# Loading chunks and weight tiles as two transfers, of partitions 0 to 119 and of 120 to 127

## The chip, the cores and the metric

The kernel runs on one core of one Trainium2 chip. The metric is the device time of one execution in microseconds (us), lower being better. Engine names are those of the profile: PE is TensorE (PEld its weight loads), DVE VectorE, ACT ScalarE, POOL GpSimd, SP SyncE, whose queue (SPq) issues every transfer of this kernel.

## What is computed

A retention layer (linear attention with a decay per head) over 4 sequences of 768 tokens with 8 heads of 64 feeds a gated feed-forward layer with a convolution of width 3:

```python
for t in range(S):                       # 768 steps, per batch and head
    state = gamma * state + outer(k[t], v[t])
    y[t] = q[t] @ state / sqrt(D)
x = y, heads side by side                # 4 x 768 x 512
h = maximum(x @ w_in, 0)                 # 512 -> 1024
conv_out[s] = sum over k of conv_w[k] * h[s + k - 1]
out = (h * sigmoid(conv_out)) @ w_out    # 1024 -> 512
```

All inputs are float32, and the two weight matrices and conv_w are float64, which the host passes as pairs of 32-bit words.

## The kernel before, in words

**Retention in chunks.** The 768 steps are cut into 12 chunks of 64 tokens; two sequences are done at a time, so there are 24 chunks in all (`n`, 0 to 23). One chunk's q, k (in two layouts) and v for two sequences and eight heads lie in a tile `rw` of 128 partitions, of which there are three. Chunks 0 to 4 are loaded in two transfers of 512 KB (`load`, L493, for q and k; `load_kv`, L497, for k and v), the later ones in one of 1 MB (L493). For a chunk, PE makes the scores (`scores`), DVE masks them (`masked`, L571), v is scaled by powers of the decay (`scale_v`: DVE at L521 or, for most chunks, ACT at L518), PE makes output and state (`mix`, all PE work of this part is at L551), ACT copies the state back (`carry`, L578), and DVE and ACT make the two halves of x, a rounded part and a rest (`decay` L585, `x_head` L595, `x_rest` L601).

**Weights.** The 16 tiles of w_in and w_out (512 KB each) and conv_w come as float64 words (`load_w`, L611) into one of four `g` tiles. ACT and DVE turn the words into two float32 parts by integer operations (`w_abs` L629 to `w_add` L710).

**Feed-forward.** For each of 12 units of 128 tokens (two sequences), `mm1` (L724) makes h from x and w_in in three products, `relu` (ACT, L733) moves it out of PSUM, DVE and ACT do the convolution and the gate (L749 to L775), and `mm2` (L789) multiplies by w_out. The result goes out by L802, 256 KB at a time.

**What sets the order.** `plan` walks through a list of tasks with estimated durations before anything is emitted and fixes the order of all instructions on each engine. It holds some transfers back so that not too many bytes queue at once (`QUEUE`, `HOLD`): such a load gets a dependency on a finished instruction of another engine (`held`, `add_manual_dep`). SP issues its transfers strictly in that order; one that waits keeps all behind it waiting. Between the tasks PE runs small filler products (`keep_warm`, L470) where the plan expects a gap. PE's own program is 37 pages of 256 instructions, which the chip fetches while the kernel runs; `Tensor.fetch` in the plan is a model of that.

**Completion counters.** Each transfer reports its landing on one of eight counters, taken in turn (DMAHW0 to DMAHW7 in the rows below). An instruction that reads the data waits for that counter, and a transfer that takes a counter again waits until the transfer that had it before has landed.

Of the kernel before, what the change touches and what calls it, by code (L numbers as in the profile page):

```python
# [11 lines left out]
I32 = mybir.dt.int32  # L12
# [32 lines left out]


PE, DVE, ACT, POOL, DMA = "PE", "DVE", "ACT", "Pool", "DMA"
ISSUE, FIRST_BYTE, SLOW_UNTIL, SLOW_BYTE, BYTE = 430, 1350, 5300, 1 / 250, 1 / 360

LANDING = {DMA: 1550, PE: 190, DVE: 130, ACT: 150, POOL: 150}  # L50
# [374 lines left out]
def retention_then_gated_ffn(  # L425
# [10 lines left out]
    nc = tc.nc  # L436
# [19 lines left out]
    def buf(name, shape, dtype=F32):  # L456
        return pool.tile(shape, dtype, name=name, bufs=BUFS[name])

    def ps_buf(name, shape=(P, 512)):
        return psum.tile(list(shape), F32, name=name, bufs=BUFS[name])  # L460
# [5 lines left out]
    def keep_warm(k):  # L466

        ps = ps_buf("ps_o")
        for i in range(k):
            nc.tensor.matmul(ps[:, : 2 * P], warm, warm.unsqueeze(1).broadcast_to([P, 2, P]), start=True, stop=True)  # L470
# [9 lines left out]
    rw, s_ps, st_ps, y_ps, xt, xs = {}, {}, {}, {}, {}, {}  # L480

    flat = lambda a: a.rearrange("p a b g c -> p a (b g c)")
    gy_0, gf, gv, mask_sb = (
        consts_sb[:, i:j].rearrange("p (a c) -> p a c", a=a) for (i, j), a in zip(CONSTS, (NPAIR, NC, NC, 1))
    )

    @emits
    def load(n):


        rw[n] = buf("rw", [P, 5, 2, NPAIR, C])
        slots = slice(0, 2 if n < ALONE else 4)
        nc.sync.dma_start(flat(rw[n][:, slots]), qkv[n][:, slots])  # L493

    @emits
    def load_kv(n):
        nc.sync.dma_start(flat(rw[n][:, 2:4]), qkv[n][:, 2:4])  # L497

    @emits
    def load_consts():  # L500
# [106 lines left out]
    @emits  # L607
    def load_w(i):
        n, src = (NF * 3, conv_w) if i == CONV else (512, w_in[i] if i < NF else w_out[i - NF])
        t = const.tile([P, 2 * n], F32, name="cw_t") if i == CONV else buf("g", [P, 2 * n])  # L610
        nc.sync.dma_start(t.bitcast(I32), src.bitcast(I32))  # L611
        t = t.rearrange("p (n w) -> p n w", w=2)
        pieces[i] = [t[:, :, 0].bitcast(I32), t[:, :, 1].bitcast(I32)]

# [189 lines left out]
    start, more, behind = plan(list_tasks())  # L804
    run_empty(WARM_UP)
    made = {}
    for k in sorted(start, key=start.get):
        if k in more:
            keep_warm(more[k])
        emit[k[0]](*k[1:])  # L810
        made[k] = nc.cur_bb.bb.instructions[-1]
        if k in behind:
            tc.add_manual_dep(
                made[k], made[behind[k]].name,
                mybir.DependencyInfo(mybir.DependencyClass.Sync, mybir.DependencyReason.DATA), reason="held back",
            )

# [50 lines left out]
```

## Time and profile before

| what | value |
|---|---|
| median of 3 runs | 351.71 us (351.38 to 360.04) |
| profiled execution | 356.1 us, its span 354.4 us |
| mean granted clock | 0.995 |
| busy: PE, PEld, DVE, ACT, POOL | 339.3, 304.9, 250.0, 207.8, 44.8 us |
| transfers | 10368 packets, 40.09 MB, 32.1% of the 16 engines' span |
| HBM read, written | 33.79 MB, 6.29 MB |

A span is the time from the first to the last instruction. Busy time is the sum of an engine's instructions; what an engine waited for is listed by line, total, number of times and longest. Transfers are listed by queue: q1 carries the kernel's data, q8 and q14 carry instructions. The median time from issue to landing stands at the end of each row of transfers. A window view gives, for each stretch, its length and then for each engine the busy time and the number of instructions, and after these the granted clock, the share of the DMA engines and GB/s.

### The profile page before, as it was taken

What the parts mean: (1) busy time and instruction counts of PE and PEld (TensorE: products, weight loads), DVE (VectorE), ACT (ScalarE), POOL (GpSimd) and SP (SyncE); (2) the same over time, 40 slices, a digit from 0 to 9 for tenths busy, and PEclk for the clock granted to TensorE, in tenths of its full rate; (3) what the DMA queues carried; (4) which work ended last, traced back from release to release, by engine and by line L of the source; (5) the groups of instructions that cost most, each with busy time, mean ns of one, the idle gap of its engine ahead of it and who ended that gap; (6) DMA issues with size and microseconds to landing.
All of it is one profiled execution on the core that took longest, in us unless ns stands there. A gap on an engine that the chain in (4) does not pass through costs nothing.

```text
span 354.4 us, 10912 instructions
## 1 busy us (share of the span) xinstructions
PE 339.3 (96%) x4763; PEld 304.9 (86%) x4763; DVE 250.0 (71%) x488; ACT 207.8 (59%) x418; POOL 44.8 (13%) x100
## 2 busy tenths in 40 slices
PE   6968999799999999999999999999999999999996
PEld 4857988799998899889888898999898888888886
DVE  3677999659999997566565675665656465999930
ACT  1255675596565887577466446446455555887831
POOL 0000000003999411000000000000000000000000
PEclk9999999899999999999999999999999999999999
DMA  7878898633020263305314334001001000100111
GB/s 249 329 254 277 283 350 308 249 120 117 18 106 0 75 227 111 100 33 179 99 42 164 120 120 148 34 2 59 4 0 62 0 31 30 61 30 31 61 59 59
DMA packets 10415, 40.78 MB, mean 115 GB/s; under 512 B 1280, under 2 KB 1664, under 8 KB 7936
## 3 DMA queue, kind: packets, MB, share of 16 engines
q1 hardware_dynamic: 10368, 40.09, 32.1%
q8 instruction: 37, 0.61, 0.7%
q14 instruction: 10, 0.08, 0.1%
HBM read 33.79 MB, written 6.29 MB: 113 GB/s over the span
## 4 chain that ended last, share of the span: by engine, by line
PE 79%; DVE 12%; issue 4%; ACT 2%; DMA 2%; SPq 0%; ACTq 0%; DVEq 0%
PE ps_o L789 35%; PE ps_m L724 30%; PE ps_y L551 5%; PE ps_st L551 4%; PE ps_s L551 4%; DVE cv L754 3%; DMA rw<-in_qkv 2%; DVE m L695 1%; DVE m L647 1%; DVE g L663 1%; DVE h L710 1%; DVE g L775 1%; DVE cv L765 1%; DVE g L655 1%; PE ps_o L470 1%
## 5 line engine op out<-in xcount | busy, mean ns | idle before, releaser
L724 PE MATMUL ps_m<-xu,wi_hi 128*128 128x256 f32 x768 | 141.6, 284 | 2.4 <-issue 2.0
L789 PE MATMUL ps_o<-h,g 128*128 128x512 f32 (+1 forms) x600 | 142.7, 386 | 0.0
L724 PEld LDWEIGHTS ps_m<-xu,wi_hi 128*128 128x128 f32 x768 | 121.4, 190 | 6.7 <-issue 0.8
L789 PEld LDWEIGHTS ps_o<-h,g 128*128 128x128 f32 x600 | 105.6, 188 | 20.0
L724 PE MATMUL ps_m<-xu,wi_lo 128*128 128x256 f32 x384 | 107.9, 281 | 0.7 <-issue 0.7
L754 DVE SCALAR_TENSOR_TENSOR cv<-h,cw_sb,cv 128x256 f32<-128x256 f32 x192 | 81.5, 480 | 16.2 <-ACT cv L749 16.2
L724 PEld LDWEIGHTS ps_m<-xu,wi_lo 128*128 128x128 f32 x384 | 72.9, 190 | 2.1 <-issue 2.1
L740 POOL COPY h<-h 128x4 f32<-128x4 f32 x80 | 43.8, 586 | 239.0 <-ACT h L733 239.0
L749 ACT ACTIVATE cv<-h,cw_sb 128x256 f32<-128x256 f32 x96 | 44.2, 503 | 18.0 <-DVE g L775 17.5
L775 DVE TENSOR_TENSOR g<-cv,g 128x512 fp32r<-128x512 f32 x48 | 33.2, 691 | 28.6 <-ACT g L770 28.3
L551 PE MATMUL ps_y<-rw 64*64 64x64 f32 x1472 | 50.2, 222 | 2.8 <-issue 2.8
L551 PEld LDWEIGHTS ps_y<-rw 64*64 64x64 f32 x1472 | 46.4, 136 | 3.9 <-issue 3.9
L760 ACT ACTIVATE cv<-cv 128x512 f32<-128x512 f32 x48 | 30.3, 632 | 24.6 <-DVE cv L754 24.5
L770 ACT CAST g<-cv 128x512 fp32r<-128x512 f32 x48 | 29.8, 621 | 24.8 <-PE ps_o L789 20.8
L765 DVE TENSOR_TENSOR cv<-h,cv 128x512 f32<-128x512 f32 x48 | 33.1, 689 | 14.4 <-ACT cv L760 13.9
L733 ACT ACTIVATE h<-ps_m 128x512 f32<-128x512 f32 x48 | 28.5, 594 | 14.6 <-PE ps_m L724 14.6
L551 PE MATMUL ps_s<-rw 64*64 64x64 f32 x768 | 29.4, 230 | 4.2 <-DMA rw<-in_qkv 2.3
L551 PEld LDWEIGHTS ps_s<-rw 64*64 64x64 f32 x768 | 26.9, 146 | 6.5 <-issue 2.4
L551 PEld LDWEIGHTS ps_st<-rw 64*64 64x64 f32 x704 | 23.8, 139 | 5.5 <-issue 3.8
L551 PE MATMUL ps_st<-rw 64*64 64x64 f32 x704 | 27.5, 226 | 0.8 <-issue 0.8
L571 DVE TENSOR_TENSOR rw<-ps_s,consts_sb 128x512 f32<-128x512 f32 x24 | 16.5, 689 | 13.4 <-PE ps_y L551 7.4
L518 ACT ACTIVATE rw<-rw,consts_sb 128x128 f32<-128x128 f32 x72 | 23.0, 392 | 4.0 <-DMA rw<-in_qkv 4.0
(39 smaller groups left out, 182.1 us busy)
## 6 DMA issues: line engine op xcount, KB each, us to landing
rw<-in_qkv SPq DMA_DIRECT2D x19, 1024.0 KB, 5.4
out_y<-o_sb SPq DMA_DIRECT2D x23, 256.0 KB, 2.0
rw<-in_qkv SPq DMA_DIRECT2D x10, 512.0 KB, 5.6
g<-in_w_in SPq DMA_DIRECT2D x8, 512.0 KB, 5.8
g<-in_w_out SPq DMA_DIRECT2D x8, 512.0 KB, 4.6
out_y<-o_sb SPq DMA_DIRECT2D x2, 128.0 KB, 1.7
consts_sb<-in_consts SPq DMA_DIRECT2D x1, 208.0 KB, 4.7
cw_t<-in_conv_w SPq DMA_DIRECT2D x1, 24.0 KB, 4.8
```

The source lines that it names most:

```text
L518: nc.scalar.activation(v[:, :, g], v[:, :, g], AF.Copy, scale=by[:, g : g + 1])
L551: nc.tensor.matmul(out, lhsT, rhs, start=start, stop=stop, skip_group_check=True)
L724: nc.tensor.matmul(h_ps[u, p][:, odd], w[:, k, fs], x[:, k].rearrange("p b t -> p (b t)"), start=(i == 0), stop=(i == len(products) - 1),)
L733: nc.scalar.activation(hs[u, p][:, :, :, 1 : P + 1], ps, AF.Relu)
L740: nc.gpsimd.tensor_copy(column(u, to), column(u + du, frm))
L749: nc.scalar.activation(cvs[u, p][:, i], hs[u, p][:, i, :, 1 : P + 1], AF.Copy, scale=cw_sb[:, f, 1:2])
L754: nc.vector.scalar_tensor_tensor(out=cv, in0=h[:, :, k : k + P], scalar=cw_sb[:, f, k : k + 1], in1=cv, op0=ALU.mult, op1=ALU.add)
L760: nc.scalar.activation(cvs[u, p], cvs[u, p], AF.Sigmoid)
L765: nc.vector.tensor_tensor(out=cv, in0=hs.pop((u, p))[:, :, :, 1 : P + 1], in1=cv, op=ALU.mult)
L770: nc.scalar.copy(gs[u, p][:, 0], cvs[u, p])
L775: nc.vector.tensor_tensor(out=lo, in0=cvs.pop((u, p)), in1=hi.bitcast(F32), op=ALU.subtract)
L789: nc.tensor.matmul(ps, g, w[f][:, cs], start=(f == 0 and i == 0), stop=(f == NF - 1 and i == 2))
```

## The change

Each load of a chunk (`load`, `load_kv`) and each load of a weight tile or of conv_w (`load_w`) becomes two transfers: one of partitions 0 to 119 and, right behind it on SP, one of partitions 120 to 127. The constants' load and the stores stay whole. The dependency of a load that is held back goes to the first of the two. The plan isn't told: its durations, and so the order of the tasks, stay.

```diff
+MOST = 120
...
+    def bring(to, src):
+
+        nc.sync.dma_start(to[:MOST], src[:MOST])
+        nc.sync.dma_start(to[MOST:], src[MOST:])
+
...
-        nc.sync.dma_start(flat(rw[n][:, slots]), qkv[n][:, slots])
+        bring(flat(rw[n][:, slots]), qkv[n][:, slots])
...
-        nc.sync.dma_start(flat(rw[n][:, 2:4]), qkv[n][:, 2:4])
+        bring(flat(rw[n][:, 2:4]), qkv[n][:, 2:4])
...
-        nc.sync.dma_start(t.bitcast(I32), src.bitcast(I32))
+        bring(t.bitcast(I32), src.bitcast(I32))
...
+        before = len(nc.cur_bb.bb.instructions)
         emit[k[0]](*k[1:])
         made[k] = nc.cur_bb.bb.instructions[-1]
         if k in behind:
             tc.add_manual_dep(
-                made[k], made[behind[k]].name,
+                nc.cur_bb.bb.instructions[before], made[behind[k]].name,
```

On SP, the start of the program before (a row is a line, the operation, the tiles and the shape; behind it the counters or engines that it waits for; the suffix _49 is part of a counter's name):

```order
1 L493 DMA rw<-in_qkv 128x1024
2 L501 DMA consts_sb<-in_consts 128x416
3 L497 DMA rw<-in_qkv 128x1024
4 L493 DMA rw<-in_qkv 128x1024
5 L497 DMA rw<-in_qkv 128x1024
6 L493 DMA rw<-in_qkv 128x1024
7 L497 DMA rw<-in_qkv 128x1024 [waits DVE_49]
```

The same place with the change, up to chunk 2's second load:

```order
1 L490 DMA rw<-in_qkv 120x1024
2 L491 DMA rw<-in_qkv 8x1024
3 L507 DMA consts_sb<-in_consts 128x416
4 L490 DMA rw<-in_qkv 120x1024
5 L491 DMA rw<-in_qkv 8x1024
6 L490 DMA rw<-in_qkv 120x1024
7 L491 DMA rw<-in_qkv 8x1024
8 L490 DMA rw<-in_qkv 120x1024
9 L491 DMA rw<-in_qkv 8x1024 [waits DMAHW0_49]
10 L490 DMA rw<-in_qkv 120x1024 [waits DMAHW1_49]
11 L491 DMA rw<-in_qkv 8x1024 [waits DMAHW2_49]
12 L490 DMA rw<-in_qkv 120x1024 [waits DMAHW3_49,DVE_49]
```

The order of the loads is the same, but the eight counters are used up with the first piece of chunk 1's second load, before with the first weight tile: row 9 waits for the first piece of chunk 0, row 11 for the constants.

On PE, the first scores before:

```order
107 L470 MATMUL ps_o<-o_sb 128x256
108 L551 MATMUL ps_s<-rw 64x64 [waits DMAHW0_49]
109 L551 MATMUL ps_s<-rw 64x64 x15
110 L470 MATMUL ps_o<-o_sb 128x256 [waits PE_49]
111 L551 MATMUL ps_s<-rw 64x64 [waits DMAHW3_49,DVE_49]
```

and with the change:

```order
107 L471 MATMUL ps_o<-o_sb 128x256
108 L557 MATMUL ps_s<-rw 64x64 [waits DMAHW0_49]
109 L557 MATMUL ps_s<-rw 64x64 [waits DMAHW1_49]
110 L557 MATMUL ps_s<-rw 64x64 x14
111 L471 MATMUL ps_o<-o_sb 128x256 [waits PE_49]
112 L557 MATMUL ps_s<-rw 64x64 [waits DMAHW5_49,DVE_49]
113 L557 MATMUL ps_s<-rw 64x64 [waits DMAHW6_49]
```

No instruction of PE, DVE, ACT or POOL changes its place; the readers of a loaded tile wait for two counters instead of one.

## The prediction

> **What bounds the kernel now.** The page comes first, for the engine that is full.
>
> ```profile
> span 354.4 us, 10912 instructions
> PE 339.3 (96%) x4763; PEld 304.9 (86%) x4763; DVE 250.0 (71%) x488; ACT 207.8 (59%) x418; POOL 44.8 (13%) x100
> PE 79%; DVE 12%; issue 4%; ACT 2%; DMA 2%; SPq 0%; ACTq 0%; DVEq 0%
> ```
>
> TensorE is busy for 339.3 of 354.4 us, and the third line, the chain that ended last, lies on it for 79%. So a change in transfers can only act where PE is idle or slow. Busy time by stage shows where that is (columns: PE, PEld, DVE, ACT, POOL, the granted clock, DMA share, GB/s).
>
> ```profile
> 0.00:66.00 66.00, 54.58 (x1495) 49.59 (x1496) 50.37 (x96) 34.64 (x76) 2.06 (x14) 1.00 0.84 289
> 66.00:70.00 4.00, 3.85 (x20) 3.85 (x20) 2.26 (x6) 1.15 (x3) 0.00 (x0) 0.57 0.80 324
> 70.00:125.00 55.00, 54.82 (x683) 51.45 (x681) 50.29 (x103) 37.37 (x75) 33.36 (x26) 1.00 0.23 77
> 125.00:355.00 230.00, 226.07 (x2572) 200.06 (x2568) 147.06 (x286) 134.59 (x266) 9.39 (x60) 1.00 0.20 70
> ```
>
> In the first 66 us PE lacks 11.4 us and the DMA share is 0.84; from 70 us on PE lacks about 0.2 us in 55 and the transfers take a fifth of the engines. The case is decided before 70 us. What PE waited for there (total, times, longest):
>
> ```profile
> PE ps_y L551 <- issue: 2.8, 5, 1.0
> PE ps_m L724 <- issue: 2.7, 2, 2.0
> PE ps_s L551 <- DMA rw<-in_qkv: 2.3, 2, 1.6
> PE ps_s L551 <- issue: 1.9, 1, 1.9
> PE ps_st L551 <- issue: 0.8, 1, 0.8
> ```
>
> Only 2.3 us are waits for a load. "issue" is time in which PE waited for nothing that the profile shows: 2.8 + 2.7 + 1.9 + 0.8 = 8.2 us in nine waits, all before 66.2 us. The longest has a sequel (a row of the chain, then the mm1 line in two windows):
>
> ```profile
> 64.18 1.97 issue
> 66.14:69.70 3.56, 3.56 (x18) 3.55 (x18) 0.52 0.85 343
> 69.70:71.70 2.00, 2.00 (x19) 2.00 (x19) 1.00 0.01 4
> ```
>
> After 1.97 us of nothing the granted clock is 0.52 for 3.56 us: 18 matmuls in 3.56 us, then 19 in 2.00 us. At full clock the 18 would have taken 18 x 2.00 / 19 = 1.90, so the sequel costs 1.7 us.
>
> The "issue" waits look like code arriving late. The DMA view of the first 66 us:
>
> ```profile
> GB/s 0 231 200 379 372 422 360 338 233 320 325 211 243 214 179 392 397 286 206 397 204 258 362 211 241 267 269 281 370 335 390 382 271 320 241 330 348 350 248 181
> DMA packets 4369, 19.08 MB, mean 289 GB/s; under 512 B 608, under 2 KB 736, under 8 KB 3424
> q1 hardware_dynamic: 4356, 18.88, 82.5%
> q8 instruction: 11, 0.18, 1.0%
> rw<-in_qkv SPq DMA_DIRECT2D x8, 1024.0 KB, 7.0
> g<-in_w_in SPq DMA_DIRECT2D x8, 512.0 KB, 5.8
> consts_sb<-in_consts SPq DMA_DIRECT2D x1, 208.0 KB, 4.7
> ```
>
> The last three rows give the loads' sizes and the us from issue to landing. Queue q8 carried 11 instruction packets of 0.18 MB / 11, about 16 KB each, while the loads kept the engines 82.5% busy. That both share engines is seen late in the run, where stores are alone but for such a packet: three windows, of 288 to 296, 268 to 273 and 304 to 308 us.
>
> ```profile
> out_y<-o_sb SPq DMA_DIRECT2D x2, 256.0 KB, 2.0
> ...
> q8 instruction: 1, 0.02, 1.5%
> out_y<-o_sb SPq DMA_DIRECT2D x1, 256.0 KB, 3.0
> ...
> q8 instruction: 1, 0.02, 2.1%
> out_y<-o_sb SPq DMA_DIRECT2D x1, 256.0 KB, 4.0
> ```
>
> A store lands in 2.0 us; with one code packet beside it, in 3.0 and 4.0. So a code packet and the rows of a data transfer queue for the same engine, and behind loads the packet is the late one. The rows do not say which engine that is.
>
> **The change part by part.** First, **the issues**. 46 loads become 92 issues.
>
> ```profile
> 0.73 0.38 SPq L493 DMA_DIRECT2D rw<-in_qkv  x1
> 1.17 0.42 SPq L501 DMA_DIRECT2D consts_sb<-in_consts  x1
> 2.11 0.43 SPq L493 DMA_DIRECT2D rw<-in_qkv  x1
> 3.08 0.71 SPq L493 DMA_DIRECT2D rw<-in_qkv  x1
> 2.11 6.97 DMA rw<-in_qkv
> 37.43 1.63 SPq L611 DMA_DIRECT2D g<-in_w_in  x2
> 42.19 2.88 SPq L611 DMA_DIRECT2D g<-in_w_in  x2
> 50.55 0.68 ACT L629 ACTIVATE m<-g 128x512 f32<-128x512 f32 x1 [1.03 <-DVE g L655]
> ```
>
> Back-to-back issues stand (2.11 - 1.17) / 2 = 0.47 us apart, with chunk 0's second load between these two. Later, SP's idle time hides the extra 46. At the start nothing does: the second piece of the first load goes out at 1.17 instead of 0.73, so the first scores are 0 to 0.47 us later; I take 0.3, since the first piece is still moving then. Chunk 1's load, the chain's 6.97 us, has three more issues up to its end, 1.4 us; the 1.2 MB queued ahead of it (at 231 GB/s some 5 us) hide those, and without that cover they cost 1.4.
>
> **The counters.** Each transfer takes the next of eight completion counters and waits for the one eight back, now four loads back instead of eight. Chunk 2's second piece waits for the constants, which landed at 1.17 + 4.7 = 5.9, so it leaves about 3 us later than chunk 2's load did at 3.08; the 2.3 MB ahead of it are still moving then and hide that. The load of weight tile 6 at 42.19 now waits for that of 37.43 to land, 5.8 us at the median: 43.2, 1 us late, with SP's next loads queued behind it. ACT first reads tile 6 at 50.55, which hides it. I take 0 for both, and 1.0 as the upper bound.
>
> **The rows per engine.** A load of 128 rows gives 16 engines 8 rows each. A 120-row piece gives its busiest engine at least 8 (over 16 or 15 engines), 15 if it gets only 8 engines; the 8-row piece adds one row to some of them. So a load's busiest engine carries 9 rows at best, 16 at worst: 9/8 to 2 times the wire time. By how the bytes are cut I take 9/8. 512 KB at the best slice, 422 GB/s, are 1.24 us, so the ninth row is 0.16 us, and 0.31 us for 1 MB. The first 66 us' share becomes 82.5 x 9/8 = 93%, still under full. Who waits for a load, beside PE's two waits above:
>
> ```profile
> ACT rw L518 <- DMA rw<-in_qkv: 4.0, 2, 2.3
> ACT m L629 <- DMA g<-in_w_in: 1.7, 1, 1.7
> ```
>
> Five waits at 0.16 to 0.31 each are 0.8 to 1.6 us, up to 2.8 if the queue at 93% adds almost as much again; some lie beside PE work. I take 1.4, bounds 0 and 2.8.
>
> The Trainium skill ("DMA: Bandwidth & Descriptors", on why a DMA increments its semaphore by 16) says that the engines used are the largest number up to 16 that divides the rows, the lowest-numbered ones: 15 for 120 rows, 8 for 8 rows. By that rule the factor is 9/8 and one engine gets no load at all; no run here shows it yet, since every transfer in this trace has 128 rows.
>
> **The code.** If code's engine still carries loads, its packets stand behind 8 or 9 rows per load. With 9, and one or two loads ahead, each of the nine waits grows by 0.16 to 0.62 us, 1.4 to 5.6 in all; with 8, by 0. I take 1.0, nearer to the lower end, as no more than about half of the loaded engines have a ninth row.
>
> The sum: 0.3 + 0 + 1.4 + 1.0 = 2.7 us. The profiled execution took 356.1 us for its span of 354.4, and becomes 358.8; it stands 4.4 us above the median of the runs, 351.7, which becomes **354.4 us**. With all lower ends it is 351.7, with all upper ones 351.7 + 0.47 + 1.0 + 2.8 + 5.6 = 361.6.
>
> **The rivals.** *Faster: the engine left without loads is the one code comes through.* Then the nine waits and the half clock go: 8.2 + 1.7 = 9.9 us. Against it: the loads still land later (+1.7 us), and DVE has little room to follow:
>
> ```profile
> 40.00:50.00 10.00, 9.85 (x288) 9.31 (x278) 9.20 (x21) 7.09 (x17) 0.68 (x5) 1.00 0.89 290
> ```
>
> With 9.20 of 10 us busy on DVE, that stretch can shrink by under 1 us. I take 2.5 us given back in all: 351.7 - 9.9 + 1.7 + 2.5 = 346.0, between 341.8 and 350. Its chance: the split may leave 0 to 8 engines of 16 without loads, 4 on average, so one in four holds the code's.
>
> *Slower: the pieces move at a worse rate than whole loads.* 19.08 MB at 422 GB/s need 45 us of the first 66, so there is room for a factor of 66 / 45 = 1.46. Above it the loads set the pace of the first stage, and the code waits vanish inside it. At 1.75 it takes 79 us, +13: 365; at 2, the end of the bound, 90 us, +24: 376. For it: 16 rows on the busiest engine, or two engines that write to the same part of SBUF and halve each other, whatever the count. Against it: in this trace 16 engines reach 422 GB/s together, but on whole loads alone.
>
> The Trainium skill ("SBUF — State Buffer", on the DMA port swizzle) says that DMA bandwidth depends on how many of 16 SBUF ports the partitions reach, four neighbouring partitions sharing one. By that rule the 8 last rows reach two ports, four engines to each, and the 120 rows may pair up too, which is a factor around or over 1.5 and so this rival's 360 to 376. The trace can't say: with 128 rows all its loads move alike.
>
> *The split changes nothing that matters*: if both pieces spread as the whole did, only the issue cost stays: 352.
>
> **How the numbers follow.** Forecast 0.40, faster rival 0.27, slower rival 0.28, no effect 0.05. Runs of this kernel differ by about 2%, so within 2% is 344.7 to 358.7. Faster: rather more than half of the faster rival, 0.15, and 0.03 for what I have not seen: 0.18. Slower: nearly all of the slower rival, 0.27, and a fifth of the forecast, 0.08: 0.35. The rest, 0.47, is within. Alone, the forecast has 351.7 to 361.6. Cases of both signs hold most of the chance, so the range reaches from 344 (about 0.1 below) to 375 (about 0.1 above).
>
> **What would show it.** Right: about nine "issue" waits of PE before 66 us summing to 8 to 13 us, a half clock near 66 us, loads landing 0.2 to 0.8 us later than 5.8 to 7.0, GB/s slices still near 400. The faster rival: "issue" waits under 2 us and a clock of 1.00 throughout. The slower one: GB/s in the first 66 us that never pass some 280, a DMA share over 0.95, and PE, ACT and DVE waiting for loads by over 10 us. The forecast is wrong if the q8 packets come on time though loads land late, or if SP's counter waits show up as PE waits for loads.

## The result, and the profile after

| | before | after |
|---|---|---|
| median of 4 runs | 352.73 us (351.38 to 360.04) | 377.24 us (373.54 to 382.74) |
| profiled span | 354.4 us | 375.2 us |
| mean granted clock | 0.995 | 0.977 |

The ratio is 1.067, with a 95% interval of 1.056 to 1.079. The kernel is slower by some 24 us. Each time given here and below is the median of all runs, slow ones among them, while a ratio and its interval compare the fast runs alone. The forecast was 354.4 us with a range of 344 to 375, so it was wrong; the time is that of the slower rival at its upper end, 376.

The page comes first again. Its transfer rows are shown too, with the number of packets by size.

```profile
span 375.2 us, 10990 instructions
PE 347.1 (92%) x4763; PEld 311.6 (83%) x4763; DVE 249.8 (67%) x488; ACT 204.8 (55%) x418; POOL 45.6 (12%) x100
DMA packets 10738, 40.79 MB, mean 109 GB/s; under 512 B 1602, under 2 KB 1986, under 8 KB 8258
q1 hardware_dynamic: 10690, 40.09, 43.0%
PE 70%; DMA 16%; DVE 5%; issue 4%; ACT 3%; SPq 1%; ACTq 0%; DVEq 0%
```

The bytes are the same, 40.09 MB, but they keep the DMA engines busy for 43.0% of a longer span, before for 32.1%. On the chain that ended last, transfers went from 2% to 16%, PE from 79% to 70% and DVE from 12% to 5%. Busy time by stage shows where (columns: stretch, length, PE, PEld, DVE, ACT, POOL, granted clock, DMA share, GB/s).

```profile
0.00:66.00 66.00, 48.08 (x1061) 43.22 (x1061) 36.19 (x65) 22.74 (x49) 0.66 (x8) 0.90 0.92 211
66.00:70.00 4.00, 2.96 (x134) 2.75 (x134) 2.57 (x6) 3.13 (x8) 0.40 (x3) 1.00 0.95 220
70.00:90.00 20.00, 14.15 (x323) 13.11 (x323) 14.34 (x31) 9.55 (x22) 0.43 (x3) 0.95 0.95 235
90.00:125.00 35.00, 35.00 (x401) 34.64 (x401) 29.42 (x60) 21.61 (x43) 18.39 (x13) 0.98 0.45 118
145.00:375.00 230.00, 227.03 (x2608) 200.99 (x2600) 147.27 (x288) 132.91 (x267) 9.54 (x60) 1.00 0.28 72
```

The last 230 us hold 227.03 us of PE work, before 226.07: nothing was lost there. The first stage, the one full of loads, ended near 66 us and now lasts to about 90. In its first 66 us the transfers move 211 GB/s instead of 289, with a DMA share of 0.92 instead of 0.84. More time on the DMA engines and fewer bytes: each transfer takes longer, and the DMA engines do not stand idle for want of transfers. The DMA view of the same 66 us (the first row is GB/s in 40 slices; the loads' rows end in KB and median us to landing):

```profile
GB/s 0 206 211 244 238 221 228 223 228 221 221 226 233 226 228 231 223 228 223 233 209 221 149 246 228 243 209 213 194 134 218 199 190 229 227 181 211 171 233 226
DMA packets 3565, 13.90 MB, mean 211 GB/s; under 512 B 653, under 2 KB 781, under 8 KB 3029
q1 hardware_dynamic: 3556, 13.76, 90.6%
q8 instruction: 8, 0.13, 1.0%
rw<-in_qkv SPq DMA_DIRECT2D x10, 480.0 KB, 9.6
rw<-in_qkv SPq DMA_DIRECT2D x5, 960.0 KB, 12.3
g<-in_w_in SPq DMA_DIRECT2D x8, 480.0 KB, 9.1
```

No slice passes 246 GB/s; before the best had 422, and fifteen were above 330. The 120 rows of a weight tile land 9.1 us after their issue, the whole tile before in 5.8. The first 19.08 MB took 66 us; now 13.90 MB come in that time, and the rest at 220 to 235 GB/s, until about 88 us. Who waited (total, times, longest), PE first:

```profile
PE ps_y L557 <- issue: 9.1, 6, 3.5
PE ps_m L730 <- issue: 6.2, 2, 3.5
PE ps_s L557 <- DMA rw<-in_qkv: 5.5, 4, 2.1
PE ps_st L557 <- issue: 2.2, 1, 2.2
PE ps_s L557 <- issue: 0.7, 1, 0.7
...
ACT rw L524 <- DMA rw<-in_qkv: 16.8, 7, 3.0
ACT m L635 <- DMA g<-in_w_in: 15.3, 5, 5.0
DVE rw L527 <- DMA rw<-in_qkv: 6.6, 3, 3.0
```

ACT waited 32.1 us for loads, before 5.7; of these, 11.7 us of `rw` come after 100 us, and all of DVE's 6.6 after 90, where PE is full and nothing is lost by them. PE itself waited only 5.5 us for them, but 9.1 + 6.2 + 2.2 + 0.7 = 18.2 us for nothing that the profile shows, in ten waits, before 8.2 in nine. None of these stands after 90 us. And the clock halves more often, in four stretches where there was one: three of about 3.4 us and one of 6.9 (same columns as the stages; the first window begins a little before the half clock does):

```profile
26.00:30.00 4.00, 4.00 (x64) 3.59 (x59) 1.69 (x4) 1.91 (x6) 0.00 (x0) 0.57 0.99 236
43.70:50.60 6.90, 5.40 (x29) 5.22 (x28) 3.93 (x8) 2.17 (x4) 0.00 (x0) 0.51 0.86 186
60.80:64.20 3.40, 3.40 (x56) 3.28 (x50) 3.12 (x7) 3.06 (x8) 0.00 (x0) 0.51 0.84 198
88.10:91.50 3.40, 3.40 (x18) 3.40 (x18) 0.43 (x1) 0.00 (x0) 0.00 (x0) 0.51 0.94 233
```

An account of the span's 20.8 us follows from the stages. PE idles 17.92 + 1.04 + 5.85 = 24.8 us up to 90 us; before it lacked 11.4 + 0.2 + 0.2 = 11.8 up to 125: 13.0 more. The mean clock loses 0.023 x 375.2 = 8.6 us, before 0.005 x 354.4 = 1.8: 6.8 more. Together that is 19.8. This is an account, and it does not say which of the waits caused another. The chain of the first 90 us says a little more:

```profile
by line: DMA rw<-in_qkv 32.4%; DMA g<-in_w_in 30.4%; PE ps_m L730 10.9%; issue 10.9%; PE ps_y L557 3.3%; PE ps_s L557 2.7%; SPq L490 2.4%; ACT m L635 2.2%; PE ps_st L557 1.4%; ACT rw L524 0.8%; SPq L491 0.7%; ACT rw L584 0.6%; ACT wi_hi L68
```

Loads have 62.8% of it, before 7.7%.

### The profile page after: what moved, and what is told of

It is laid out like the page before. It is cut to its first block, busy times and chain, and to the rows that moved or that the text cites. A ratio compares the mean times of both kernels' runs of the same rounds, so it can differ in the third digit from the quotient of the medians.

```text
span 375.2 us, 10990 instructions
## 1 busy us (share of the span) xinstructions
PE 347.1 (92%) x4763; PEld 311.6 (83%) x4763; DVE 249.8 (67%) x488; ACT 204.8 (55%) x418; POOL 45.6 (12%) x100
## 2 busy tenths in 40 slices
DMA packets 10738, 40.79 MB, mean 109 GB/s; under 512 B 1602, under 2 KB 1986, under 8 KB 8258
## 3 DMA queue, kind: packets, MB, share of 16 engines
q1 hardware_dynamic: 10690, 40.09, 43.0%
## 4 chain that ended last, share of the span: by engine, by line
PE 70%; DMA 16%; DVE 5%; issue 4%; ACT 3%; SPq 1%; ACTq 0%; DVEq 0%
PE ps_o L795 36%; PE ps_m L730 26%; DMA rw<-in_qkv 8%; DMA g<-in_w_in 7%; PE ps_s L557 3%; PE ps_st L557 3%; PE ps_y L557 3%; DMA g<-in_w_out 1%; DVE m L653 1%; DVE g L669 1%; DVE m L701 1%; ACT rw L524 1%; ACT m L635 1%; SPq L490 1%; DVE h L716 1%
## 5 line engine op out<-in xcount | busy, mean ns | idle before, releaser
L730 PE MATMUL ps_m<-xu,wi_hi 128*128 128x256 f32 x768 | 144.7, 288 | 2.9 <-issue 2.7
L730 PEld LDWEIGHTS ps_m<-xu,wi_hi 128*128 128x128 f32 x768 | 123.8, 194 | 9.2 <-ACT m L635 3.5
L730 PE MATMUL ps_m<-xu,wi_lo 128*128 128x256 f32 x384 | 109.3, 285 | 3.5 <-issue 3.5
L730 PEld LDWEIGHTS ps_m<-xu,wi_lo 128*128 128x128 f32 x384 | 74.4, 194 | 2.8 <-issue 2.8
L746 POOL COPY h<-h 128x4 f32<-128x4 f32 x80 | 44.7, 596 | 257.4 <-ACT h L739 257.4
L557 PE MATMUL ps_y<-rw 64*64 64x64 f32 x1472 | 52.1, 225 | 9.1 <-issue 9.1
L557 PEld LDWEIGHTS ps_y<-rw 64*64 64x64 f32 x1472 | 47.8, 138 | 10.3 <-issue 10.3
L771 DVE TENSOR_TENSOR cv<-h,cv 128x512 f32<-128x512 f32 x48 | 33.2, 692 | 19.8 <-ACT cv L766 19.3
L557 PE MATMUL ps_s<-rw 64*64 64x64 f32 x768 | 32.3, 237 | 6.3 <-DMA rw<-in_qkv 5.5
L557 PEld LDWEIGHTS ps_s<-rw 64*64 64x64 f32 x768 | 29.1, 151 | 9.1 <-DMA rw<-in_qkv 3.7
L557 PEld LDWEIGHTS ps_st<-rw 64*64 64x64 f32 x704 | 24.6, 141 | 7.0 <-issue 5.4
L577 DVE TENSOR_TENSOR rw<-ps_s,consts_sb 128x512 f32<-128x512 f32 x24 | 16.5, 689 | 19.1 <-PE ps_s L557 11.1
```

Source lines behind the costliest of these rows:

```text
L557: nc.tensor.matmul(out, lhsT, rhs, start=start, stop=stop, skip_group_check=True)
L730: nc.tensor.matmul(h_ps[u, p][:, odd], w[:, k, fs], x[:, k].rearrange("p b t -> p (b t)"), start=(i == 0), stop=(i == len(products) - 1),)
L746: nc.gpsimd.tensor_copy(column(u, to), column(u + du, frm))
L771: nc.vector.tensor_tensor(out=cv, in0=hs.pop((u, p))[:, :, :, 1 : P + 1], in1=cv, op=ALU.mult)
```

## The experiments

Three things could make the pieces slow: which partitions a transfer reaches, how many DMA engines carry it, or how many transfers and counters there are. A second question was the code, which the forecast and the faster rival saw in opposite ways. `after` stands below for the changed kernel. Edits are to its `bring` or to the calls of it. The time behind "against" is that of the kernel before, run beside the variant.

### The rates of pieces, by themselves

A kernel of loads alone: per stage eight loads of 8 KB rows into eight tiles, the next stage's loads behind the end of it (shortened).

```python
def stage(pieces):
    for i in range(8):
        for p in pieces:
            nc.sync.dma_start(tiles[i][p], src[frm])
    end_of_stage()
```

> Not the reference's computation: it only loads, in twelve stages of eight transfers each (rows of 8 KB, q, k and v of a chunk, into eight tiles), each stage starting when the one before has landed whole; the output is zeros. Stages: 128 rows twice, 120 rows, the last 8 rows, 120 + 8, 64 rows, 64 rows by twos (partitions 0, 2, 4 ... 126), 16 rows, 16 rows by eights (partitions 0, 8 ... 120), 96, 112, 128 rows. Theory 1 (a transfer's rows are dealt to engines so that two engines write to the same part of SBUF at once, and each then goes at half rate): 128 rows near 400 GB/s, 120 rows alone near 220, 120 + 8 a little under that, 64 neighbouring rows near 210, 16 neighbouring rows near 100 but 16 spread rows near 200. Theory 2 (more transfers, each with its own fixed cost and counter, are what is slow): 120 rows alone 15/16 of the rate of 128, so near 380, only 120 + 8 near 220. Theory 3 (the 8-row piece alone blocks eight engines): 120 rows near 380, 8 rows alone under 60 GB/s, 120 + 8 near 220.

Measured, one row per stage (stretch, length, DVE and POOL busy, granted clock, DMA share, GB/s). In order: 128 rows (the second of two such stages); 0 to 119; 120 to 127; both pieces; 0 to 63; every second of 128; 0 to 15; every eighth of 128; 0 to 95; 0 to 111; 128 again, with the first stores beside them.

```profile
42.40:64.78 22.38, 0.00 (x0) 0.00 (x0) 1.00 0.91 375
65.66:105.34 39.68, 0.00 (x0) 0.00 (x0) 1.00 0.88 198
106.62:117.63 11.01, 0.01 (x2) 0.00 (x0) 1.00 0.37 48
118.51:163.31 44.80, 0.01 (x1) 0.00 (x0) 1.00 0.86 187
164.10:186.90 22.80, 0.00 (x0) 0.00 (x0) 1.00 0.89 184
187.78:201.66 13.88, 0.00 (x0) 0.00 (x0) 1.00 0.76 302
202.54:213.66 11.12, 0.00 (x0) 0.00 (x0) 1.00 0.76 95
214.54:221.91 7.37, 0.00 (x0) 0.00 (x0) 1.00 0.51 142
222.79:249.82 27.03, 0.00 (x1) 0.00 (x0) 1.00 0.92 233
250.70:277.98 27.28, 0.00 (x1) 0.00 (x0) 1.00 0.92 269
278.86:302.88 24.02, 0.00 (x0) 0.00 (x0) 1.00 0.95 378
```

The two pieces take 44.80 / 22.38 = 2.0 times the whole load's time. Of the 22.4 us more, the 120 rows alone already cost 17.3, and the 8 rows behind them 5.1. Equal numbers of rows differ by where they lie: 64 neighbours take 22.80 us, as long as 128 rows, and 64 rows spread by twos 13.88; 16 neighbours 11.12 us, spread by eights 7.37. Both kinds read rows that lie together in memory, so what counts is which partitions the rows reach. That is theory 1 as far as it can be seen: no row shows which engine writes where, so that two of them write to the same part of SBUF stays an inference. For 16 spread rows the theory gave too much, near 200 GB/s, and 142 were measured. That the 8-row piece is the whole cost, or that a row more per engine is, is excluded: they would have left the 120 rows near the whole load's rate, and these move 198 GB/s. The small packets of the stage of whole loads and of that of 120 rows tell how many engines a load runs on, if each engine that takes part adds one:

```profile
DMA packets 1152, 8.39 MB, mean 375 GB/s; under 512 B 128, under 2 KB 128, under 8 KB 128
DMA packets 1080, 7.86 MB, mean 198 GB/s; under 512 B 120, under 2 KB 120, under 8 KB 120
```

That is 16 for each of eight whole loads and 15 for each of 120 rows. One engine in 16 fewer is far from a rate of half.

### The same with PE running, and smaller products after

To see which engine carries PE's code, nine such stages (128, 120+8, 120, 126, 117, 108, 121, 100 and 128 rows), while PE runs 6000 products that wait for none of the loads.

```diff
+    for i in range(PRODUCTS):
+        nc.tensor.matmul(ps[:64, :64], zero[:64, :64], zero[:64, :64], start=True, stop=True)
```

> Not the reference's computation: nine stages of eight loads each, of 128, 120 + 8, 120, 126, 117, 108, 121, 100 and 128 rows, while PE runs 6000 small products of a zero tile with no wait between them, so that its only waits are those for its code; the output is zeros. If 120 rows go to 15 engines, 126 to 14, 117 to 13, 108 to 12, 121 to 11 and 100 to 10 (the largest number up to 16 that divides the rows), PE's issue waits go away from the first stage on that leaves the code's engine free. Theory A (the 16th engine carries the code, and 120 + 8 did free it): long issue waits in the 128-row stages alone, none from 120 + 8 on. Theory B (the code's engine is one of those that 120 + 8 still loads): waits of many us in the stages of 128, 120 + 8 and 120 rows, then none below some number of rows; that number tells the engine. Theory C (code waits for transfers whatever engine they use): waits in all stages.

Measured: 1285.48 us, and over the whole run one wait of PE, for the zeros that it multiplies.

```profile
PE ps L62 <- DVE zero L29: 1.4, 1, 1.4
```

This tells nothing. The products took 1285 / 6000 = 0.2 us each, so PE used up its code too slowly to run out of it. The next kernel had 9000 smaller ones, bf16 zeros with a result of 32x32, and a stage of 88 rows more, behind that of 100.

```diff
+    few = zero.bitcast(mybir.dt.bfloat16)[:, :32]
...
-        nc.tensor.matmul(ps[:64, :64], zero[:64, :64], zero[:64, :64], start=True, stop=True)
+        nc.tensor.matmul(ps[:32, :32], few, few, start=True, stop=True)
```

> Not the reference's computation: ten stages of eight loads each, of 128, 120 + 8, 120, 126, 117, 108, 121, 100, 88 and 128 rows, while PE runs 9000 tiny products of about 0.03 us (so a page of code lasts about 4 us) with no wait but for code; the output is zeros. In the first try PE's products were 0.2 us long and it never ran out of code. Theory A (the engine that 120 + 8 leaves free is the code's): issue waits in the stages of 128 rows alone. Theory B (the code's engine is loaded by 120 + 8 as well): issue waits of 15 us and more in each of the stages of 128, 120 + 8 and 120 rows, and almost none in some stage of fewer engines (100 rows, if 10 engines, or 117). Theory C (code waits for transfers on any engine): issue waits of 10 us and more in all ten stages.

Measured, PE's waits in four of the stages, in order 128 rows, 120+8, 120 and 88 (total, times, longest; one answer for each stage):

```profile
PE ps L63 <- issue: 8.5, 4, 3.1
...
PE ps L63 <- issue: 22.6, 5, 6.4
...
PE ps L63 <- issue: 23.0, 5, 5.4
...
PE ps L63 <- issue: 9.5, 4, 4.8
```

Between them 126 rows had 15.5 us of waits, 117 11.1, 108 8.7, 121 13.6, 100 9.9, and the last 128 rows 8.6. That these are waits for code shows in PE's rows, one before the first load and two of the 120+8 stage:

```profile
11.04 6.80 PE L63 MATMUL ps<-zero 128*32 128x32 bf16 x256 [0.28 <-issue]
57.75 3.58 PE L63 MATMUL ps<-zero 128*32 128x32 bf16 x128 [6.41 <-issue]
66.69 3.57 PE L63 MATMUL ps<-zero 128*32 128x32 bf16 x128 [5.36 <-issue]
```

PE stops after 128 products or a multiple of them, and 128 products with their weight loads are one page of 256 instructions. Without loads a page is 0.28 us late, beside the pieces 5.36 and 6.41.

No stage is free of waits, though five of the ten have less than the 10 us that theory C expected. The faster rival's mechanism falls: the 120 rows alone leave one engine of 16 without loads, and PE waited 23.0 us. The full rate is better for the code than the pieces are, 8.5 us against 22.6. But the rate alone does not set the waits: the stage of 121 rows lasts as long as that of 120+8, 43.4 us each, and has 13.6 us. By its small packets, 88 for eight loads, it ran on 11 engines, and the 100 rows, with 80, on 10. With 100 rows six of the eight waits are of 0.33 to 1.20 us, while with 120 every wait but the first is over 5. That would fit code that comes over several engines in turn, some of them free in those stages; no run tests it. Which engine or engines carry the code stays open.

### Two transfers, all 128 partitions in both

Each row is cut in the middle instead, so there are as many transfers, counters and issues as in `after`, but each reaches all partitions.

```diff
-        nc.sync.dma_start(to[:MOST], src[:MOST])
-        nc.sync.dma_start(to[MOST:], src[MOST:])
+        for i in range(2):
+            part = lambda t: t[(slice(None),) * (len(t.shape) - 1) + (slice(i * t.shape[-1] // 2, (i + 1) * t.shape[-1] // 2),)]
+            nc.sync.dma_start(part(to), part(src))
```

> Each load is again two transfers, but each of all 128 partitions and half of every row, so 46 more issues, counters four loads back and two waits per tile as in the change, with whole columns of partitions. Theory 1 and theory 3 (rate of pieces with fewer rows): 351 to 356 us, within 1% of before. Theory 2 (number of transfers, issues, counters): 370 to 380 us as with the change.

Measured: 356.33 us against 354.47, ratio 1.005 (1.000 to 1.009). With loads that reach all partitions, issues and counters are worth at most 0.009 x 354.5 = 3.2 us; the prediction's first two terms had 0.3, and 1.5 at their upper ends.

### Two halves of partitions, neighbouring or interleaved

```diff
-        nc.sync.dma_start(to[:MOST], src[:MOST])
-        nc.sync.dma_start(to[MOST:], src[MOST:])
+        nc.sync.dma_start(to[:64], src[:64])
+        nc.sync.dma_start(to[64:], src[64:])
```

> Each load is two transfers, of partitions 0 to 63 and of 64 to 127: the same count of transfers, and 4 rows for each of 16 engines in both. Theory 1: 64 neighbouring rows move at half rate, two engines to each part, GB/s never over 230 in the first 66 us, 372 to 390 us. Theory 2: about 377 us too. Theory 3 (only a piece of 8 rows blocks): 351 to 357 us.

Measured: 378.18 us against 354.47, ratio 1.061 (1.051 to 1.070). Its counterpart has the even and the odd partitions:

```diff
-        nc.sync.dma_start(to[:MOST], src[:MOST])
-        nc.sync.dma_start(to[MOST:], src[MOST:])
+        nc.sync.dma_start(to[0::2], src[0::2])
+        nc.sync.dma_start(to[1::2], src[1::2])
```

> Each load is two transfers of 64 partitions, the even ones and the odd ones: the same rows per transfer, the same number of transfers and engines as in the split at 64, which took about 1.06 of before. Theory 1 (what counts is which partitions the engines write at the same time; the stage of 64 partitions by twos moved 4 MB in 13.9 us, that of 64 neighbouring ones in 22.8): 352 to 358 us, like the split by columns. Theory 2 (rows per transfer or engines' shares, wherever they lie): 372 to 385 us, like the split at 64.

Measured: 356.36 us against 354.92, ratio 1.004 (1.000 to 1.008). The first 66 us and the packets of both, of the neighbouring halves first:

```profile
0.00:66.00 66.00, 47.88 (x1191) 42.95 (x1192) 38.87 (x71) 26.25 (x57) 1.70 (x11) 0.97 0.96 222
DMA packets 11152, 40.79 MB, mean 109 GB/s; under 512 B 2016, under 2 KB 2400, under 8 KB 8672
```

and of the interleaved ones:

```profile
0.00:66.00 66.00, 56.23 (x1494) 51.17 (x1494) 48.56 (x92) 32.99 (x73) 2.75 (x14) 0.97 0.83 284
DMA packets 11152, 40.79 MB, mean 115 GB/s; under 512 B 2016, under 2 KB 2400, under 8 KB 8672
```

Both have the same transfers, sizes, issues and packets, down to the 2016 small ones. Only the partitions differ (and the rows read, every second one in the interleaved case; the stages alone read rows that lie together and show the same), and with them 222 or 284 GB/s and nearly the whole loss. This pair decides it: the loss comes from the partitions that a piece reaches, not from there being pieces. By what path the slow loads reach PE differs. In the neighbouring halves, loads have only 15.5% of the chain of the first 90 us, and waits of PE for nothing that the profile shows 23.1%; in `after` it was 62.8% and 10.9%.

### Only the weights, only the chunks

```diff
-        bring(flat(rw[n][:, slots]), qkv[n][:, slots])
+        nc.sync.dma_start(flat(rw[n][:, slots]), qkv[n][:, slots])
...
-        bring(flat(rw[n][:, 2:4]), qkv[n][:, 2:4])
+        nc.sync.dma_start(flat(rw[n][:, 2:4]), qkv[n][:, 2:4])
```

> Only the 17 loads of weight tiles and conv_w are split at 120; the chunks come whole. Theory 1 with a first stage that has room: 6.3 MB at 225 GB/s (28 us) and 12.8 MB at 400 (32 us) are 60 of 66 us, so little is lost: 353 to 360 us. If instead every split load costs its reader a fixed delay: 17 of 46 loads, some 361 us.

Measured: 362.21 us against 354.92, ratio 1.019 (1.010 to 1.028). That is above the 353 to 360 of theory 1 and near the 361 of a fixed delay for each load. The other way round:

```diff
-        bring(t.bitcast(I32), src.bitcast(I32))
+        nc.sync.dma_start(t.bitcast(I32), src.bitcast(I32))
```

> Only the 29 loads of chunks are split at 120; weights come whole. Theory 1: 12.8 MB at 225 GB/s (57 us) and 6.3 MB at 400 (16 us) are 73 us against 66, so the first stage grows by 7 to 12 us: 359 to 366 us. With a fixed delay for each split load: 29 of 46 loads, some 368 us.

Measured: 375.98 us against 354.92, ratio 1.062 (1.055 to 1.070). That is nearly the whole loss from the chunks alone, 10 us above the upper end of theory 1 and 8 above the 368 of a fixed delay. Its first stage, and its GB/s in 40 slices of the first 66 us:

```profile
0.00:66.00 66.00, 46.90 (x1188) 42.47 (x1189) 38.07 (x70) 26.53 (x57) 1.54 (x11) 0.88 0.92 226
66.00:90.00 24.00, 17.32 (x342) 16.55 (x342) 14.64 (x31) 9.25 (x21) 0.35 (x3) 0.90 0.95 220
GB/s 0 203 210 211 245 236 243 238 236 238 278 328 216 214 169 196 216 236 290 223 204 171 335 278 216 199 139 223 218 194 142 377 261 223 223 164 273 345 223 211
```

By 90 us it has moved 226 x 66 + 220 x 24 = 20.2 MB, hardly more than the 19.5 of `after`, although its weight tiles come as whole loads. I had let the weights keep their own full rate for the whole of their time. Some slices reach 328 to 377 GB/s, where `after` had none over 246, so whole loads do go faster for moments. But the DMA engines were as busy as in `after` and moved little more, so whole loads and pieces side by side took longer than apart. Which of the two lost, the rows do not tell. One at a time the two cost 7 and 21 us, together 24; with these intervals the difference from their sum means nothing.

### Only the late loads

```diff
+        (bring if n >= 12 else nc.sync.dma_start)(flat(rw[n][:, slots]), qkv[n][:, slots])
...
+        nc.sync.dma_start(flat(rw[n][:, 2:4]), qkv[n][:, 2:4])
...
+        (bring if i >= 11 and i < CONV else nc.sync.dma_start)(t.bitcast(I32), src.bitcast(I32))
```

> Only the 17 loads issued from about 63 us on are split at 120 (chunks 12 to 23, weight tiles 11 to 15); the 29 before come whole. Theory 1 with a full first stage as the place: no cost beyond 1%, 352 to 358 us, since transfers take a fifth of the engines there. If each split load costs its readers a fixed delay: about 17 of 46 of the loss, 361 us.

Measured: 355.78 us against 353.88, ratio 1.003 (0.997 to 1.008). Seventeen loads issued from about 63 us on cost nothing that can be measured, at most 0.008 x 354 = 2.8 us. The fixed delay for each load, which would have given 361, is excluded with that: the loss arises where loads are dense.

### A cut at 112

```diff
-MOST = 120
+MOST = 112
```

> Each load is two transfers, of 112 and of 16 partitions, both over 16 engines by the rule, so no engine is left out. From the stages measured alone (eight transfers of 112 rows 27.3 us, of 16 rows 11.1 us, together 4.8 us a load, against 5.6 for 120 + 8 and 2.8 for whole loads) theory 1 expects between the two, nearer to the change: 364 to 374 us. If the 15 and 8 engines are what costs: 351 to 357 us.

Measured: 371.02 us against 353.88, ratio 1.052 (1.044 to 1.060), as expected. Its first 66 us move 243 GB/s, between `after`'s 211 and the 289 of whole loads; the 112 rows by themselves had moved 269 where 120 had 198. If the 15 and 8 engines were the cost, 351 to 357 us should have come out: here both pieces run on 16. The kernels follow the rates measured alone as far as their intervals tell them apart: 0 to 119 with 8, 1.067; 0 to 63 with 64 to 127, 1.061; 0 to 111 with 16, 1.052; evens with odds, 1.004. PE's waits for nothing that the profile shows go along: 18.2, 20.6, 15.8 and 7.7 us, with the chunks alone 17.4, with the weights alone 12.9, and before 8.2.

## Why the prediction was wrong, point by point

**The step that failed** is "By how the bytes are cut I take 9/8", the factor on a load's wire time, with 1.4 us for it. Measured by itself the factor is 44.80 / 22.38 = 2.0, the upper end of the bound. In the kernel the best slice fell from 422 to 246 GB/s, and the 19.08 MB of the first 66 us took until about 88. The bound ended at 2 because of 16 rows on one engine, which is not what happened; the slower rival's time came out because its other cause, halving, gives the same 2. I counted rows per engine, as if each engine moved a row in the same time wherever it goes. The stages of equal size exclude that: 64 rows take 22.80 or 13.88 us by their places. That the DMA share came out near the forecast's 93%, at 90.6%, was luck: it was reached with 13.76 MB in place of 18.88. The trace of before had only loads of 128 partitions, so the rate of 422 GB/s was known for one shape only, and I carried it to another.

**What stood against it was in the prediction.** The port rule of the Trainium skill ("SBUF — State Buffer", on the DMA port swizzle) was cited there with a factor of around or over 1.5. By that rule partitions 0 to 63 reach 8 of 16 ports; the trace agrees, with 184 GB/s for them and 302 for 64 partitions by twos. But 120 partitions reach all 16 by that rule and still moved at 198 GB/s, so the number of ports reached is not all that counts. The Trainium skill ("DMA: Bandwidth & Descriptors", on the descriptor swizzle) adds that in a transfer of 128 partitions each engine writes one port of its own. With that, every shape other than 128 should have been doubted, and the slower rival given more than 0.28.

**The engines.** "16 rows on the busiest engine" was not the reason. In the kernel before, 72 transfers made 16 small packets each, beside conv_w's 128 rows: 1280. In `after` it is 1602 = 26 x 16 + 46 x (15 + 8) + 128, so a piece of 120 rows ran on 15 engines, which makes 8 rows for each, and a piece of 8 on 8 engines. This is the count that the prediction gave by the Trainium skill ("DMA: Bandwidth & Descriptors", on why a DMA increments its semaphore by 16), and it was right. What the forecast left out is that 15 engines with 8 rows each may write to the same parts of SBUF; the slower rival had it. That this is what happens with 120 rows is inferred from the 64- and 16-row stages; how the rows are dealt to the engines was not measured.

**Issues and counters**, 0.3 and 0, were sized well as far as can be told: the row halves, with the same issues and counters, gave a ratio of 1.005. In `after` SP did wait 17.5 us of the first 90 for a load to land, before not at all. But the neighbouring halves cost as much with 1.7 us of such waits, so they follow from the slow loads and are not the price.

**The code**, 1.0 us, was undersized: PE's waits for nothing that the profile shows grew from 8.2 to 18.2 us, +10.0, above the 5.6 of its upper end, and the half clock from one stretch to four. The mechanism, code late behind loads, is borne out by the stages with PE running: a page is 0.28 us late without loads, the waits are 8.5 us at the full rate and 22.6 behind the pieces. The price was small because it was worked out with the factor 9/8, for rows on one engine.

**The rivals.** The slower one was right in its time, 376, and in its deciding factor: 2.0 is above 1.46, and the loads set the pace of the first stage. Of its two causes 16 rows on an engine is excluded, and engines that share a part of SBUF fits all that was measured but the sharing itself was not seen. Its signs came for the most part: no slice past 280 GB/s, and waits for loads of 20.4 us on ACT in the first 90 us. PE's 5.5 us and a DMA share of 0.92 to 0.95 stayed under what it named. Wrong in it was that "the code waits vanish inside it"; they more than doubled. The faster rival fell with the 120 rows alone, which leave an engine without loads and had the most code waits, 23.0 us. "No effect" fell with the rates.

**The frame held.** "The case is decided before 70 us" is what the late loads showed (1.003), though the first stage now ends near 90, and the last 230 us kept their PE work to within 1 us.

## What to carry to other kernels

A DMA rate read from loads of all 128 partitions need not hold for a load of fewer: 375 and 198 GB/s here. Before a tile is cut along the partitions, measure the pieces by themselves in a kernel of loads alone, and if a load must be cut, cut along the free dimension or interleave the partitions. And where transfers slow down, look at what else queues behind them: here the busiest engine waited longer for its code than for its data, 10.0 us more against 3.2.

## What the runs showed of the hardware that was not expected

- 64 neighbouring partitions took as long to load as 128 (22.80 and 22.38 us), though half the bytes.
- 96 and 112 partitions were slow as well, at 233 and 269 GB/s beside 375 for 128. Their exact order by the number of rows is not explained by any run.
- Whole loads and slow pieces side by side moved little more than pieces alone: 226 GB/s over the first 66 us with the weights whole, 211 with none. Single slices reached 377.
- PE waited for code in every stage with loads in flight, even with 88 rows (9.5 us in 35), where by the small packets only 11 engines carry loads.
- The clock halved in `after` three times for about 3.4 us and once for 6.9. A wait of PE of 2.2 to 3.5 us stands just before or at the start of each; that it is the cause was read from the order in the trace, not tested.
